# Pooled attention with a bilinear expert layer: eight blocks transposed on TensorE, half of the weight magnitudes on ScalarE

## The chip, the cores and the metric

One core of a Trainium2 chip runs the whole program. The metric is device time in microseconds, the median of the runs of one kernel.

## The reference

Attention over B, H, S, D = 4, 8, 1152, 64 with queries averaged in pairs (576 per head), then a bilinear layer on 2304 tokens of 512 features:

```python
q_pool = q.reshape(B, H, S // 2, 2, D).mean(axis=3)
scores = q_pool @ k.transpose(0, 1, 3, 2) / sqrt(D)
attn = exp(scores - max(scores)); attn = attn / (sum(attn) + 1e-09)
x = (attn @ v), heads side by side        # 2304 x 512
out = ((x @ w_a) * (x @ w_b)) @ w_out     # 512 -> 1536 -> 512
```

The layer's three weights are taken in a raw form of 64-bit words (two 32-bit words for each number), out of which the kernel makes the number itself.

## The kernel before, in words

**Attention.** Heads go in 16 pairs (two heads on the two halves of the 128 partitions), four pairs to a batch. A pass works on one pair; in batch 0 a pass takes only the even or the odd half of its queries. A pass is cut into blocks of 128 queries of one head (an even pass has 4 blocks, an odd one 5 with the rest of 64 queries). For a block: TensorE makes the scores (`qk`, L657 in f32 for the first batches, L660 from f16 halves later), VectorE scales them out of PSUM into `s` and takes the maximum (`sm_max`, L692), ScalarE takes the exponential with its sum (`sm_exp`, L699), VectorE the reciprocal of the sum (L703, L709), ScalarE divides and rounds to f16 (`sm_hi`, L712), VectorE makes the f16 remainder (`sm_lo`, L716), and SP issues a DMA transpose of both halves into `pt` (`transpose`, L722). Two blocks make a unit: TensorE multiplies `pt` by the split v (`pv`, L752), ScalarE copies the result out of PSUM (`x_copy`, L761).

**Weights.** 36 tiles (12 column groups f, each of w_a, w_b and w_out) are loaded (`w_load`, L539), their high word made a magnitude on ScalarE (`w_abs`, L545), the low word converted on ScalarE (`w_tail`, L558), the sign put in on POOL (`w_sign`, L562) and the two joined on VectorE (`w_join`, L569). For w_a and w_b a maximum over the tile gives the scale: VectorE `w_max` (L551) ahead of the join, a shift `w_mag` (L577), a sum over partitions on TensorE (`w_sum`, L583), the scale (L586) and its reciprocal (L591). Then the tile is split into two f16 parts (`w_hi`, L607, and `w_lo`, L611). All of this belongs to the first passes.

**The MoE stage.** For each of 9 token tiles and each f, TensorE multiplies x with w_b and w_a into `ab0` or `ab1` (`moe_mm`, L830; the same two PSUM tiles under the names `acc0` and `acc1` take the second product, `moe_o`, L856), ScalarE and VectorE form the product g (L837, L842), and g is split (L847, L850) for the second product. Tile 0 needs all four even passes and its weights.

**What sets the order.** Every step is added with its engine, its tiles read and written; the order of each engine's list is written out as numbers in ORDERS, one list for each of TensorE, VectorE, ScalarE, POOL and SP. Each engine goes through its list strictly in order.

Of the kernel before, what the change touches and what calls it, by code (L numbers as in the profile page):

```python
# [10 lines left out]
I32 = mybir.dt.int32  # L11
# [17 lines left out]
REMN = 64  # L29
N_WHOLE, TWO_ROUNDS = 2, (0,)  # L30
# [55 lines left out]
    ),  # L86
    (
# [215 lines left out]
def kernel(  # L303
# [46 lines left out]
    vsc = T("vsc", [128, NPAIR, 3])  # L350
    vb = T("vb", [128, B, 2])
    wmx = T("wmx", [128, NF, 2])
    wal = T("wal", [128, NF, 2])
    wsc = T("wsc", [128, 2, NF, 2])
    cc = T("cc", [128, B, NF, 2])

# [292 lines left out]
    def sbuf(i):  # L649
        return i % NS  # L650
# [429 lines left out]
```

## Time and profile before

| | us |
|---|---|
| median of 3 runs | 851.35 |
| lowest, highest run | 850.94, 855.6 |
| the profiled execution's own time | 852.03 |
| its span, first to last instruction | 849.8 |

The profile page gives busy time by engine, and forty equal slices (21.25 us each) in tenths of busy time; PEclk is TensorE's granted clock in tenths of full speed (0.5 is 1.2 GHz, full is 2.4 GHz). PE is TensorE, PEld its weight load, DVE VectorE, ACT ScalarE, POOL GpSimd, SP SyncE. L12 is line 12 of the kernel.

### The profile page before, as it was taken

The page shows a single profiled execution, that of the slowest core. Times are in us where ns is not written, and L with a number is a line of the kernel's source. Part 1 is how long each engine was busy: PE and PEld are TensorE (multiplying, and loading weights), DVE is VectorE, ACT ScalarE, POOL GpSimd, SP SyncE. Part 2 cuts the span into 40 slices and gives each one's busy share as a digit, 9 for nine tenths or more (in the row PEclk, how much of TensorE's full clock was granted, in tenths as well). Part 3 has the DMA queues.
Part 4 walks back from the last instruction along what each step waited for, and adds up shares of the span by engine and source line. Part 5 has one row for each costly group of instructions (what it writes and reads, how often), then busy time and mean ns, then how long its engine had stood idle before and what let it go on. Part 6 is the DMA issues. An engine that isn't in the chain of part 4 may idle for free.

```text
span 849.8 us, 21268 instructions
## 1 busy us (share of the span) xinstructions
PE 771.8 (91%) x8832; PEld 591.2 (70%) x8832; DVE 644.9 (76%) x1240; ACT 580.9 (68%) x929; POOL 255.1 (30%) x230
## 2 busy tenths in 40 slices
PE   4665546999999999999999999999999999999998
PEld 2343324676767777778777777787788778888886
DVE  5999999987988889899999999999866744132110
ACT  5798888877778778888888788777756644233222
POOL 3666677651240022302051113111301321201203
PEclk8755767999999999999999999999999999999999
DMA  8999899999999999999999999996965743300100
GB/s 286 233 246 263 225 222 231 270 180 228 204 208 196 192 217 188 196 191 207 161 215 195 189 193 171 168 200 142 182 159 111 116 93 57 57 27 1 25 1 25
DMA packets 353664, 141.76 MB, mean 167 GB/s; under 512 B 338208, under 2 KB 340256, under 8 KB 353568
## 3 DMA queue, kind: packets, MB, share of 16 engines
q1 hardware_dynamic: 353568, 140.40, 81.5%
q8 instruction: 69, 1.13, 0.5%
q14 instruction: 27, 0.22, 0.1%
HBM read 50.72 MB, written 4.72 MB: 65 GB/s over the span
## 4 chain that ended last, share of the span: by engine, by line
PE 53%; DVE 2%; DMA 1%; issue 1%; ACT 0%
PE ab L830 24%; PE ab L856 14%; PE sps L660 8%; PE xps L752 7%; DMA pt<-p 1%; DVE p L716 1%; DVE s L692 1%; DVE g L842 0%; ACT g L837 0%; PE xps L485 0%; DVE vs L518 0%; DVE vmx L481 0%; DVE o L862 0%; PE xps L418 0%; DVE st L709 0%
## 5 line engine op out<-in xcount | busy, mean ns | idle before, releaser
L830 PEld LDWEIGHTS <-wab 128*128 128x128 f16 x2592 | 252.4, 98 | 35.2 <-issue 2.3
L830 PE MATMUL ab<-xt,wab 128*128 128x256 f16 x2304 | 262.3, 274 | 3.2 <-DVE g L842 3.2
L716 DVE SCALAR_TENSOR_TENSOR p<-s,st,p 128x1152 f16<-128x1152 f32 x144 | 206.7, 1439 | 20.1 <-ACT p L712 19.4
L712 ACT ACTIVATE p<-s,st 128x1152 f16<-128x1152 f32 x144 | 178.4, 1248 | 44.8 <-DVE st L709 13.5
L699 ACT ACTIVATE s<-s,st 128x1152 f32<-128x1152 f32 x144 | 179.6, 1248 | 34.6 <-DVE s L692 34.4
L850 POOL TENSOR_TENSOR gl<-g,gh 128x256 fp32r<-128x256 f32 x108 | 94.0, 877 | 328.9 <-ACT gh L847 295.0
L657 PE MATMUL sps<-k,q 64*128 64x512 f32 (+3 forms) x448 | 117.5, 620 | 56.5 <-DVE s L692 36.6
L856 PE MATMUL ab<-wo,gh 128*128 128x512 f32 x432 | 140.0, 405 | 1.7 <-DVE g L842 1.7
L657 PEld LDWEIGHTS sps<-k,q 64*128 64x128 f32 (+1 forms) x448 | 54.0, 210 | 118.8 <-issue 62.9
L752 PE MATMUL xps<-pt,vs 128*64 128x128 f16 (+1 forms) x4320 | 127.4, 219 | 6.6 <-DMA pt<-p 3.8
L752 PEld LDWEIGHTS <-vs 128*64 128x64 f16 x4320 | 117.8, 113 | 19.3 <-issue 16.0
L837 ACT ACTIVATE g<-ab,cc 128x256 f32<-128x256 f32 (+1 forms) x144 | 55.6, 416 | 97.4 <-PE ab L830 97.2
L692 DVE TENSOR_SCALAR_CACHE_REDUCE s<-sps,ksc 128x1152 f32<-128x1152 f32 x72 | 101.0, 1411 | 12.0 <-PE sps L660 11.2
L842 DVE SCALAR_TENSOR_TENSOR g<-ab,cc,g 128x256 f32<-128x256 f32 (+1 forms) x144 | 56.0, 412 | 70.4 <-ACT g L837 70.3
L692 DVE TENSOR_SCALAR_CACHE_REDUCE s<-sps 128x1152 f32<-128x1152 f32 x72 | 96.8, 1349 | 7.7 <-PE sps L657 7.1
L856 PEld LDWEIGHTS ab<-wo,gh 128*128 128x128 f32 x432 | 77.8, 188 | 20.1 <-ACT g L837 1.5
L856 PE MATMUL ab<-wo,gl 128*128 128x512 f32 x216 | 85.5, 396 | 0.0
L847 ACT ACTIVATE gh<-g 128x256 fp32r<-128x256 f32 x108 | 43.4, 411 | 48.5 <-PE ab L856 47.7
L660 PE MATMUL sps<-k,q 64*128 64x512 f16 (+3 forms) x624 | 65.4, 341 | 0.0
L660 PEld LDWEIGHTS <-q 64*128 64x128 f16 (+1 forms) x720 | 36.6, 97 | 39.9 <-issue 7.4
L562 POOL TENSOR_SCALAR xt<-xt 128x512 f16<-128x512 f32 x22 | 53.9, 2449 | 22.0 <-ACT xt L558 17.0
L856 PEld LDWEIGHTS ab<-wo,gl 128*128 128x128 f32 x216 | 40.6, 188 | 10.1 <-POOL gl L850 0.4
(99 smaller groups left out, 626.2 us busy)
## 6 DMA issues: line engine op xcount, KB each, us to landing
k<-in_k_dram SPq DMA_DIRECT2D x19, 576.0 KB, 4.8
vraw<-in_v_dram SPq DMA_DIRECT2D x19, 576.0 KB, 4.7
xt<-in_w_ab_dram SPq DMA_DIRECT2D x15, 512.0 KB, 4.8
qraw<-in_q_dram SPq DMA_DIRECT2D x12, 576.0 KB, 4.7
out_dram<-o SPq DMA_DIRECT2D x16, 256.0 KB, 2.5
xt<-in_w_out_dram SPq DMA_DIRECT2D x7, 512.0 KB, 4.4
g<-in_w_ab_dram SPq DMA_DIRECT2D x5, 512.0 KB, 5.1
pt<-p SPq DMA_TRANSPOSE x144, 5.5
```

Source lines behind the costliest of these rows:

```text
L657: nc.tensor.matmul(out, q, k, start=True, stop=True)
L660: nc.tensor.matmul(out, q[:, hq], k[:, hk], start=(hq, hk) == (0, 0), stop=(hq, hk) == (1, 0))
L692: nc.vector.tensor_scalar(out=s_t[sbuf(i)], in0=sps[:, at:at + S], scalar1=-1.0 / 16.0 if u is None else ksc[:, u, 4:5], scalar2=None, op0 ...
L699: nc.scalar.activation(out=s, in_=s, func=AF.Exp, scale=-1.0, bias=t[:, 0:1], accum_out=t[:, 1:2])
L712: nc.scalar.activation(out=p_t[pbuf(i)][:, 0], in_=s_t[sbuf(i)], func=AF.Copy, scale=st_t[i % NST][:, 3:4])
L716: nc.vector.scalar_tensor_tensor(out=p[:, 1], in0=s, scalar=st_t[i % NST][:, 3:4], in1=p[:, 0], op0=ALU.mult, op1=ALU.subtract)
L752: nc.tensor.matmul(xps[half(e), at:at + w], vs[:, c, e, hv], pt[:, hp, c, c0:c0 + w], start=(c == 0 and n == 0), stop=(c == NCH - 1 and n ...
L830: nc.tensor.matmul(dst if t < 8 else dst.rearrange("p (b n) -> p b n", b=B), wab[:, f, 1 - m, a, c], moe_x(t, b, c), start=(n == 0), stop= ...
L837: nc.scalar.activation(out=g_t[:, f, c], in_=ab[j][:, 1, c], func=AF.Copy, scale=cc[:, b, f, 0:1])
L842: nc.vector.scalar_tensor_tensor(out=g, in0=ab[j][:, 0, c], scalar=cc[:, b, f, 1:2], in1=g, op0=ALU.mult, op1=ALU.mult)
L850: nc.gpsimd.tensor_tensor(out=gl_t[j], in0=g_t[:, f], in1=gh_t[j].bitcast(F32), op=ALU.subtract)
L856: nc.tensor.matmul(acc[u], g[:, us], wo[:, f, a], start=(first and n == 0), stop=(last and n == 2))
```

## The change

1. The blocks of the first two passes (two head pairs, even halves: 8 blocks) have no `sm_hi`, `sm_lo` and DMA transpose. The undivided exponentials `s` are transposed in 128 x 128 pieces on TensorE into `acc0` and `acc1` (9 pieces a block, in groups of 4, or of 2 where the last pieces of two blocks go together), and split from PSUM: ScalarE `tr_hi`, VectorE `tr_lo`. The division follows behind p times v: the reciprocals of the sums are put on the diagonal of a 128 x 128 tile (`r_diag`, ScalarE), spread over the partitions by a matmul (`r_wide`), and multiplied in (`r_mul`, VectorE). `x_copy` then takes 128 columns at a time for these passes.
2. The weight magnitude is taken behind the join. For even f a VectorE reduction (maximum of magnitudes), for odd f a ScalarE pass that sums the magnitudes. The shift of the maxima is gone.
3. An identity is made on POOL once (`unity`).
4. All five order lists are new.

```diff
+N_PE = 2
-    def w_max(f, m, n):
-        z = z_t[zi(n)]
-        nc.vector.tensor_scalar(
-            out=z, in0=z, scalar1=2.0 ** -126, scalar2=None, op0=ALU.max, op1=ALU.max, accum_out=wmx[:, f, m:m + 1]
-        )
+    def w_mag(f, m, n):
+        if on_act(f):
+            nc.scalar.activation(out=w_dst(f, m, 0), in_=w_src(m, n), func=AF.Abs, accum_out=wmx[:, f, m:m + 1])
+        else:
+            z = z_t[zi(n)]
+            nc.vector.tensor_reduce(
+                out=wmx[:, f, m:m + 1], in_=z, axis=AX.X, op=ALU.max, apply_absolute_value=True
+            )
-    def w_mag(f):
-        nc.vector.tensor_scalar(
-            out=wal[:, f].bitcast(I32), in0=wmx[:, f].bitcast(I32), scalar1=3, scalar2=None, op0=ALU.logical_shift_left
-        )
...
+    def tr_pe(chunks, j):
+        for n, (i, c) in enumerate(chunks):
+            nc.tensor.transpose(acc[j][:, 128 * n:128 * n + 128], s_t[sbuf(i)][:, 128 * c:128 * c + 128], ident)
+    def tr_hi(chunks, j):
+        nc.scalar.activation(out=tr_dst(chunks, 0), in_=tr_src(chunks, j), func=AF.Copy, scale=P_SCALE)
+    def tr_lo(chunks, j):
+        nc.vector.scalar_tensor_tensor(
+            out=tr_dst(chunks, 1), in0=tr_src(chunks, j), scalar=P_SCALE, in1=tr_dst(chunks, 0),
+            op0=ALU.mult, op1=ALU.subtract,
+        )
+    def r_diag(i, e):
+        nc.scalar.activation(out=diag[e], in_=ident, func=AF.Copy, scale=st_t[i % NST][:, 3:4])
+    def r_wide():
+        for e in range(2):
+            nc.tensor.matmul(
+                xps[half(e), 256:384], one.broadcast_to([128, 64]), diag[e], start=True, stop=True
+            )
+    def r_mul(j, x0):
+        x = x32[j][:, x0:x0 + 128]
+        nc.vector.tensor_tensor(out=x, in0=x, in1=xps[:, 256:384], op=ALU.mult)
...
+        if ps_.pe:
+            e = blocks[i].head
+            add("ACT", 0.19, i - 3, r_diag, (i, e), r=[t + "r", "g0"], w=[f"g{1 + e}"])
+            return
         add("ACT", 1.15, i - 3.5, sm_hi, (i,), r=[s, t + "r"], w=[p + "h"])
```

What stands ahead of the first MoE step in the lists, before and after. VectorE, ahead of the first `moe_g`: `sm_max` 25 and 23, `sm_lo` 23 and 13, `w_max` 22 and none, shifts 11 and none, `w_join` 31 and 30, `w_lo` 18 and 18, reductions none and 10, `tr_lo` none and 20, `r_mul` none and 4. ScalarE, ahead of the first `moe_a`: `sm_exp` 24 and 22, `sm_hi` 23 and 13, `w_abs` and `w_tail` 32 and 30 each, `w_hi` 28 and 26, `x_copy` 4 and 6, `tr_hi` none and 20, `r_diag` none and 8, magnitudes none and 8. TensorE, ahead of the first `moe_mm`: `qk` entries 25 and 23, `pv` 8 and 8, `tr_pe` groups none and 20, `r_wide` none and 4. SP issues 144 and 136 transposes in all.

## Rows read from the trace of the kernel before

**Rows 1.** The page: span, TensorE's share, then its slices, clock and DMA.

```profile
span 849.8 us, 21268 instructions
PE 771.8 (91%) x8832; PEld 591.2 (70%) x8832; DVE 644.9 (76%) x1240; ACT 580.9 (68%) x929; POOL 255.1 (30%) x230
...
PE   4665546999999999999999999999999999999998
...
PEclk8755767999999999999999999999999999999999
DMA  8999899999999999999999999996965743300100
```

**Rows 2.** Busy time by stretch: start:end us, length, then engines (instructions), clock, DMA.

```profile
0.00:150.00 150.00, 84.91 (x651) 51.89 (x652) 134.08 (x274) 118.71 (x175) 97.91 (x55) 0.69 0.98 244
150.00:210.00 60.00, 54.42 (x715) 40.50 (x714) 50.45 (x97) 46.85 (x72) 23.35 (x18) 0.97 1.07 228
210.00:780.00 570.00, 567.54 (x7047) 444.33 (x7041) 452.63 (x855) 399.49 (x647) 117.76 (x137) 1.00 0.85 159
```

**Rows 3.** TensorE's timeline where the MoE stage starts: start us, us, instruction.

```profile
143.33 3.86 PE L657 MATMUL sps<-k,q 64*128 64x512 f32 x10 [3.69 <-DVE s L692]
147.12 1.48 PE L830 MATMUL ab<-xt,wab 128*128 128x256 f16 x12
```

**Rows 4.** Waits from 0 to 160 us: total us, times, longest.

```profile
PE sps L657 <- DVE s L692: 34.6, 17, 3.7
...
ACT xt L558 <- DMA xt<-in_w_ab_dram: 4.6, 1, 4.6
...
PE xps L752 <- DMA pt<-p: 3.1, 3, 1.8
```

**Rows 5.** VectorE's groups from 0 to 150 us: busy us, mean ns, idle before.

```profile
L692 DVE TENSOR_SCALAR_CACHE_REDUCE s<-sps 128x1152 f32<-128x1152 f32 x25 | 33.7, 1348 | 2.8 <-PE sps L657 2.6
L716 DVE SCALAR_TENSOR_TENSOR p<-s,st,p 128x1152 f16<-128x1152 f32 x22 | 31.7, 1446 | 0.8 <-ACT p L712 0.7
...
L551 DVE TENSOR_SCALAR_CACHE_REDUCE o<-o 128x512 f32<-128x512 f32 x9 | 6.1, 676 | 3.9 <-ACT o L545 3.9
...
L481 DVE TENSOR_REDUCE vmx<-vraw 128x1 f32<-128x1152 f32 x4 | 5.4, 1340 | 0.0
...
L577 DVE TENSOR_SCALAR wal<-wmx 128x2 int32<-128x2 int32 x10 | 4.5, 454 | 0.0
...
L551 DVE DVE_READ_ACCUMULATOR o<-o 128x1 f32 x9 | 0.7, 82 | 0.0
```

**Rows 6.** ScalarE's groups from 0 to 150 us.

```profile
L699 ACT ACTIVATE s<-s,st 128x1152 f32<-128x1152 f32 x24 | 29.9, 1246 | 7.2 <-DVE s L692 7.2
L712 ACT ACTIVATE p<-s,st 128x1152 f16<-128x1152 f32 x23 | 28.3, 1244 | 5.8 <-DVE st L709 4.4 <-issue 1.4
...
L545 ACT ACTIVATE o<-xt 128x512 f32<-128x512 f32 x9 | 5.8, 649 | 2.1 <-DMA xt<-in_w_ab_dram 2.1
...
L699 ACT ACTIVATION_READ_ACCUMULATOR s<-s,st 128x1 f32 x24 | 4.5, 187 | 0.0
...
L761 ACT ACTIVATE x<-xps 128x256 f32<-128x256 f32 x4 | 1.4, 361 | 0.0
```

**Rows 7.** Single lines that read PSUM, whole span: ns min/median/max.

```profile
L864 ACT ACTIVATE o<-ab x9: 575/598/601, 258.8 to 845.4; 128x512 f32<-128x512 f32 x9
...
L862 DVE COPY o<-ab x9: 674/689/692, 256.8 to 846.1; 128x512 f32<-128x512 f32 x9
...
L842 DVE SCALAR_TENSOR_TENSOR g<-ab,cc,g x144: 274/475/485, 153.5 to 829.1; 128x256 f32<-128x256 f32 x96, 128x64 f32<-128x64 f32 x48
```

**Rows 8.** TensorE's timeline: one pair of scores and one rest, full clock.

```profile
99.67 2.20 PE L657 MATMUL sps<-k,q 64*128 64x512 f32 x10
...
152.61 0.48 PE L657 MATMUL sps<-k,q 64*128 64x128 f32 x2
```

**Rows 9.** POOL's timeline at the start.

```profile
5.62 0.72 POOL L408 TENSOR_TENSOR q<-qraw 128x256 f32<-128x256 f32 x1 [5.18 <-DMA qraw<-in_q_dram]
```

More of the change, by code (lines that the diff above doesn't have):

```diff
@@ L352 @@
     wmx = T("wmx", [128, NF, 2])
-    wal = T("wal", [128, NF, 2])
     wsc = T("wsc", [128, 2, NF, 2])
@@ L387 @@
     kzf = [x.bitcast(F16).rearrange("p (a n) -> p a n", a=2) for x in kz]
+    ident, diag = g_t[:, 0, 0:128], [g_t[:, 1 + e, 0:128] for e in range(2)]
     pl = Plan()
@@ L547, in w_abs, with on_act @@
         )
-    def w_max(f, m, n):
-        z = z_t[zi(n)]
-        nc.vector.tensor_scalar(
-            out=z, in0=z, scalar1=2.0 ** -126, scalar2=None, op0=ALU.max, op1=ALU.max, accum_out=wmx[:, f, m:m + 1]
-        )
+    def on_act(f):
+        return f % 2 == 1
+    def w_mag(f, m, n):
[6 more added lines that the diff above has]
+            )
     def w_tail(n):
@@ L574, in w_ones @@
         nc.vector.memset(one, 1.0)
-    def w_mag(f):
-        nc.vector.tensor_scalar(
-            out=wal[:, f].bitcast(I32), in0=wmx[:, f].bitcast(I32), scalar1=3, scalar2=None, op0=ALU.logical_shift_left
-        )
     def w_sum(f):
-        nc.tensor.matmul(sums, one.broadcast_to([128, 128]), wal[:, f], start=True, stop=True)
+        nc.tensor.matmul(sums, one.broadcast_to([128, 128]), wmx[:, f], start=True, stop=True)
     def w_scale(f):
         nc.vector.tensor_scalar(
-            out=wsc[:, 1, f], in0=sums, scalar1=2.0 ** -100, scalar2=2.0 ** -14, op0=ALU.max, op1=ALU.mult
+            out=wsc[:, 1, f], in0=sums, scalar1=2.0 ** -100, scalar2=2.0 ** -15, op0=ALU.max, op1=ALU.mult
         )
@@ L625, in prep_w @@
             add("ACT", 0.55, key, w_abs, (n,), r=[rw], w=[z])
-            if m < 2:
-                add("DVE", 0.6, key, w_max, (f, m, n), w=[z, f"wmx{f}{m}"])
             add("ACT", 0.555, key, w_tail, (n,), w=[rw + "l"], r=[rw])
@@ L630, in prep_w @@
             add("DVE", 0.68, key, w_join, (n,), r=[rw, rw + "l"], w=[z], port=True)
+            if m < 2:
+                last = [f"z{NZ + m}"] if f == NF - 1 else []
+                last += ["raw2"] if f == NF - 2 else []
+                if on_act(f):
+                    add("ACT", 0.66, key, w_mag, (f, m, n), r=[z], w=[f"wmx{f}{m}", f"w{f}{m}h"] + last)
+                else:
+                    add("DVE", 0.6, key, w_mag, (f, m, n), r=[z], w=[f"wmx{f}{m}"])
             if m == 1:
-                add("DVE", 0.07, key, w_mag, (f,), r=[f"wmx{f}0", f"wmx{f}1"], w=[f"wal{f}"])
-                add("PE", 0.2, key - 5, w_sum, (f,), r=[f"wal{f}", "ones"], w=["xps"])
+                add("PE", 0.2, key - 5, w_sum, (f,), r=[f"wmx{f}0", f"wmx{f}1", "ones"], w=["xps"])
                 add("DVE", 0.07, key - 5, w_scale, (f,), r=["xps"], w=[f"wsd{f}"])
@@ L725, in transpose, with unity, tr_dst @@
         )
+    def unity():
+        nc.gpsimd.memset(ident, 0.0)
+        nc.gpsimd.affine_select(
+            out=ident, in_=ident, compare_op=ALU.not_equal, fill=1.0, base=0, pattern=[[-1, 128]], channel_multiplier=1
+        )
+    def tr_pe(chunks, j):
+        for n, (i, c) in enumerate(chunks):
+            nc.tensor.transpose(acc[j][:, 128 * n:128 * n + 128], s_t[sbuf(i)][:, 128 * c:128 * c + 128], ident)
+    def tr_dst(chunks, hl):
+        i, c = chunks[0]
+        c0 = 128 * blocks[i].slot
+        if chunks[1][0] == i:
+            return pt[:, hl, c:c + len(chunks), c0:c0 + 128]
+        return pt[:, hl, c, c0:c0 + 256]
@@ new lines, in tr_src @@
+    def tr_src(chunks, j):
+        x = acc[j][:, 0:128 * len(chunks)]
+        return x.rearrange("p (c n) -> p c n", n=128) if chunks[1][0] == chunks[0][0] else x
+    def tr_hi(chunks, j):
[5 more added lines that the diff above has]
+        )
@@ new lines, in r_diag, with moved @@
+    def r_diag(i, e):
[4 more added lines that the diff above has]
+                xps[half(e), 256:384], one.broadcast_to([128, 64]), diag[e], start=True, stop=True
+            )
+    def r_mul(j, x0):
+        x = x32[j][:, x0:x0 + 128]
+        nc.vector.tensor_tensor(out=x, in0=x, in1=xps[:, 256:384], op=ALU.mult)
+    def moved(ps_, i0, u):
+        slots = [blocks[i].slot for i in (i0, i0 + 1)]
+        parts = [[(i, c + d) for d in range(4)] for i in (i0, i0 + 1) for c in (0, 4)] + [[(i0, 8), (i0 + 1, 8)]]
+        for n, chunks in enumerate(parts):
+            j = n % 2 if u % 2 == 0 else (n + 1) % 2
+            of = sorted(set(i for i, _ in chunks))
+            names = [f"pt{blocks[i].slot}x{chunks[0][1]}" for i in of]
+            add("PE", 0.05 + 0.17 * len(chunks), i0 - 6, tr_pe, (chunks, j), r=[f"s{sbuf(i)}" for i in of] + ["g0"], w=[f"acc{j}"])
+            add("ACT", 0.08 + 0.107 * len(chunks), i0 - 3.5, tr_hi, (chunks, j), r=[f"acc{j}"], w=[x + "h" for x in names])
+            add("DVE", 0.1 + 0.14 * len(chunks), i0 - 3.5, tr_lo, (chunks, j), r=[f"acc{j}"] + [x + "h" for x in names], w=[x + "l" for x in names])
+        return [f"pt{t}x{c}{hl}" for t in slots for c in (0, 4, 8) for hl in "hl"]
@@ L758, in pv, with x_copy, unit @@
                     )
-    def x_copy(j, at, x0, w):
-        nc.scalar.activation(out=x32[j][:, x0:x0 + w], in_=xps[:, at:at + w], func=AF.Copy, scale=1.0 / P_SCALE)
-    def unit(slots, at, w, key):
+    def x_copy(j, at, x0, w, scale):
+        nc.scalar.activation(out=x32[j][:, x0:x0 + w], in_=xps[:, at:at + w], func=AF.Copy, scale=scale)
+    def unit(slots, at, w, key, parts):
         runs = [128 * t for t in slots] if len(slots) > 1 else [128 * slots[0], 128 * slots[0] + w]
-        add("PE", 0.04 + 1.49 * w / 128, key - 9, pv, (runs, at, w), r=[f"pt{t}" for t in slots] + ["vsh", "vsl"],
+        add("PE", 0.04 + 1.49 * w / 128, key - 9, pv, (runs, at, w), r=[f"pt{t}" for t in slots] + ["vsh", "vsl"] + parts,
             w=["xps"], mode=2)
@@ L769, in leave @@
         j = ps_.jx
-        add("ACT", 0.072 + 0.192 * w / 256, key - 4, x_copy, (j, at, x0, w), r=["xps"],
-            w=[f"x32{j}{c}" for c in range(x0 // 64, (x0 + w) // 64)])
+        add("ACT", 0.072 + 0.192 * w / 256, key - 4, x_copy, (j, at, x0, w, P_SCALE ** -2 if ps_.pe else 1.0 / P_SCALE),
+            r=["xps"], w=[f"x32{j}{c}" for c in range(x0 // 64, (x0 + w) // 64)])
+        if ps_.pe:
+            add("DVE", 0.22, key - 4, r_mul, (j, x0), r=["xps"], w=[f"x32{j}{c}" for c in range(x0 // 64, (x0 + w) // 64)])
     def x_parts(p, j, which, hl):
@@ L926, in __init__ @@
             self.whole = b > 0
+            self.pe = n < N_PE
             self.split = b >= N_WHOLE
@@ L978 @@
     add("DVE", 0.2, -30, w_ones, (), w=["ones"])
+    add("POOL", 0.8, -30, unity, (), w=["g0"], port=False)
     prep_qk(passes[0], -20)
@@ L1002, in attend @@
                 prep_vmax(nxt.p, nxt.parts[0] == "even", ps_.end - 4)
-            unit(slots, at, w, i - 1)
+            parts = moved(ps_, i - 2, r) if ps_.pe else []
+            unit(slots, at, w, i - 1, parts)
+            if ps_.pe:
+                add("PE", 0.3, i - 9, r_wide, (), r=["g1", "g2", "ones"], w=["xps"], mode=2)
+                leaving = [(at, XE + at, 128)]
             for span in leaving:
```

285 rows, old and new, of the table ORDERS are left out of this document.

## The prediction

> **What bounds the kernel now.** I read the page first. TensorE is busy for 771.8 of 849.8 us, and its granted clock is below full only in the first seven of the forty slices [rows 1]. So the next view is busy time by stretch [rows 2]. From 210 to 780 us TensorE works 567.5 of 570 us at full clock: whatever it has to do there is paid in full, and nothing else in that stretch can shorten the run. The first 150 us are different: TensorE is busy 84.9 us at a mean clock of 0.69, VectorE 134.1 us and ScalarE 118.7 us. This is the start-up, in which 36 weight tiles are joined and split while the first head pairs are attended. It ends when the first matmuls of the MoE stage enter, at 147.1 us, behind a scores product that was itself waiting for VectorE [rows 3]. From there TensorE is full (54.4 of 60 us in the stretch that follows).
>
> Who holds the start-up is in the waits: TensorE waits 34.6 us for VectorE's scaled copy with maximum, in 17 waits, but only 3.1 us for transposed probabilities, and ScalarE 4.6 us for weight loads [rows 4]. The DMA engines are nearly full there too (0.98), but hardly anybody waits for them: the bound is VectorE, 89% busy, with ScalarE at 79% behind it.
>
> So the time is (when the MoE stage starts) + (work that TensorE still has to do). The profiled execution took 852.03 us for its span of 849.8, and the median of the runs is 851.35; I take differences from that execution and apply them to the median.
>
> **The change, part by part.**
>
> *Eight blocks without DMA transpose.* For each, VectorE loses a sm_lo of 1.446 us [rows 5] and ScalarE a sm_hi of 1.244 us [rows 6]. In their place come 20 groups (16 of 512 columns, 4 of 256) that are read from PSUM: tr_lo on VectorE, tr_hi on ScalarE. Nearest rows, also PSUM to SBUF: VectorE 0.689 us for 512 columns and 0.475 for 256 (the median, which is the 256-column form), ScalarE 0.598 for 512 [rows 7] and 0.361 for 256 [rows 6]. So tr_lo costs 16 x 0.689 + 4 x 0.475 = 12.9 us against 8 x 1.446 = 11.6, and tr_hi 16 x 0.598 + 4 x 0.361 = 11.0 us against 10.0: neither engine gains by this part alone. The division that moves behind p times v adds 4 r_mul of 128 columns to VectorE, between 0.08 (a one-column reading) and 0.475 us: I take 0.31, 1.2 us. On ScalarE 8 r_diag of 128 columns lie between 0.187 and 0.361: I take 0.28, 2.2 us. The copies out of PSUM are now 8 of 128 columns instead of 4 of 256: about 8 x 0.28 - 4 x 0.361 = 0.8 us.
>
> *TensorE.* 72 transposes of 128 x 128 and four r_wide. No row shows a transpose. The nearest is the f32 product on 128 columns, two instructions in 0.48 us [rows 8]. A transpose costs between 0.1 us (if loads and streams overlap) and 0.48; I take one instruction of the pair, 0.24 us, together 17 us, and 7 to 35 for the range. All of it is ahead of the first MoE step in TensorE's list, so it falls into the 65 us in which TensorE idles by 150 us and is costed at nothing. If that cover were gone (half clock, see the rivals), it would be paid in full.
>
> *DMA.* Eight transposes leave SP's queue. Its engines move less, but since the waits for them are a few us, I count nothing for it; weight loads may land earlier, which is a reason for a gain beyond my value, none for a loss.
>
> *Weight magnitude.* VectorE loses 24 w_max of 0.676 + 0.082 us and 12 shifts of 0.454 us: 18.2 + 5.4. It gains 12 reductions of 512 columns. The reduction over 1152 columns took 1.340, as long per column as the instruction it replaces, so I take 0.676 (0.60 by simple proportion): 8.1 us. ScalarE gains 12 magnitudes, each a 512-column pass of 0.649 and an accumulator read of 0.187: 10.0 us. The magnitude is now behind the join in its chain (sign on POOL, join, magnitude), so scales come later for a tile; what hides this is that tiles are joined long before the MoE stage needs them.
>
> *unity on POOL* stands first in its list, where POOL waits 5.18 us for the first queries [rows 9]: nothing.
>
> *Sum over all parts.* VectorE: -11.6 - 18.2 - 5.4 + 12.9 + 8.1 + 1.2 = -13.0 us. ScalarE: -10.0 + 11.0 + 2.2 + 10.0 + 0.8 = +14.0 us. Work moves from the engine that bounds the start-up to the one behind it.
>
> *Order.* The lists are written anew, so what counts is the work that stands ahead of the first MoE step, by the counts that the text gives with the diff. VectorE: 2 sm_max of 1.43 fewer (-2.9), 10 sm_lo fewer (-14.5), 22 w_max (-16.7) and 11 shifts (-5.0) gone; 20 tr_lo (+12.9), 10 reductions (+6.8), 4 r_mul (+1.2) added: -18.2 us, 134.1 becomes 115.9. ScalarE: 2 sm_exp with readings fewer (-2.9), 10 sm_hi fewer (-12.4), 2 each of w_abs, w_tail and w_hi fewer (-3.9 at 0.649); 20 tr_hi (+11.0), 8 r_diag (+2.2), 8 magnitudes (+6.7), 6 small copies for 4 (+0.2): +0.9 us, 118.7 becomes 119.6. The two are now level.
>
> When does the MoE stage start? If one engine alone sets it, at VectorE's 89%, ScalarE's 119.6 us give 134 us, 16 earlier. If the two keep the joint rate that they have now (252.8 us of work in 150), 235.5 us take 139.7: 10.3 earlier. I take the second, since a block passes from one to the other several times and two level engines wait on each other more than one full and one slack engine. Against this, two entries of scores (one pair of 2.20 and one rest of 0.48 at full clock [rows 8]) are no longer done in the start-up but in the full stretch: +2.7. **Net -7.6 us: 851.35 - 7.6 = 843.7 us.** By the profiled execution itself it would be 844.4.
>
> **The rivals.**
>
> *A, a larger gain.* One engine sets the pace, or the lighter DMA lets weights land early: start at 134 us, -16 + 2.7 = -13, 838 us or somewhat less. For it: the DMA share of 0.98. Against: those small waits.
>
> *B, no change.* ScalarE's idle 31 us of 150 are not VectorE's fault, and with no less work on it the stage starts where it did. Then the two moved scores cost 2.7 and what VectorE saves becomes idle: 851 to 854. For it: ScalarE's work ahead of the MoE stage does not fall. Against: the waits that rank first are for VectorE.
>
> *C, slower: two PSUM buffers.* All 20 groups pass through the same two tiles, acc0 and acc1. A group's buffer is free again only after four transposes, the tr_hi and the tr_lo, and each engine keeps its order: a tr_lo that waits holds back the sm_max behind it, and so TensorE's next scores. If each group leaves VectorE idle for 1 us, the start comes 20 us later than forecast: 851.35 - 7.6 + 20 = 863.8. It decides from 7.6 / 20 = 0.38 us per group on. Against: VectorE's list puts a sm_max, a join or a magnitude between most groups.
>
> *D, slower: TensorE at half clock becomes the bound.* In the start-up TensorE already runs for long stretches at 1.2 GHz (a tenth between 5 and 10 is a mixture of the two levels, 1.2 and 2.4 GHz) [rows 1]. Its 84.9 us at 0.69 are 58.6 us at full clock, 117 at half; less the moved scores (5.4 at half), with transposes of 17 us, that is 129 us, and if the 34.6 us of waits for VectorE stay, the stage starts at 164: +14 + 2.7, 868 us. For it: the clock's digit is 5 in slices three and four already. Against: TensorE will idle less, not more. The Trainium skill, TensorE: Matmul & The Clock Gate, section on the PE-mode transpose, speaks for D: it says that the full clock does not engage for matmuls in transpose mode, and gives about 275 ns for one of bf16 in a kernel, by which 72 would take 20 us (an estimate from that page). No run here shows either so far.
>
> **How the numbers follow.** The forecast of -7.6 gets 0.48, A 0.16, B 0.19, C 0.12, D 0.05. A change of under 0.5% (4.3 us, 847.1 to 855.6) is about what a measurement of this kernel cannot tell from none. All of A and the forecast lie below it: 0.64 faster; B is within it: 0.19; C and D are above: 0.17. The likeliest case's own range is 838 to 847, by the two ways to reckon the start and by TensorE's bounds. To hold the time 8 times in 10 the range takes A's value and B: 836 to 854; out remain C, D and the far end of A.
>
> **What would show it.** Right: the first MoE matmuls at about 140 us instead of 147 (137 to 143); VectorE near 116 us busy by then and ScalarE near 120; TensorE's waits for sm_max well below 34.6 us; the stretch behind as full as before. The new rows should read: tr_lo 0.69, tr_hi 0.60, a transpose near 0.24 us. Wrong: if the stage starts at 147 or later with VectorE idle in front of tr_lo, it is C; with ScalarE at 85% and more and VectorE waiting for it, B; with a clock near 0.5 and TensorE busy throughout, D. If the start is earlier but the time is not, then TensorE must idle later, in the 60 us after the start, where more weight tiles than before are still to be split.

## The result, and the profile after

The changed kernel takes 841.03 us (median of 4 runs, 836.85 to 841.74) against 853.48 for the kernel before on the same chips; ratio 0.9848, 95% interval 0.9806 to 0.989. The forecast was faster, 843.7 us, 0.9% below the median; it came out 1.5% below. Measured again beside the experiments, the kernel before took 851.69, 851.87 and 850.98 us (medians of 25, 31 and 9 runs), so against those the gain is 10 to 11 us and not 12.4. The profiled execution is the fastest of the runs, 836.85 us for a span of 835.1, so of the 14.7 us between the spans of the two traces a few are not the change's; the medians decide.

The page of the changed kernel: span, busy share, TensorE's slices (20.9 us each), clock and DMA, against [rows 1].

```profile
span 835.1 us, 21457 instructions
...
PE 773.5 (93%) x8920; PEld 595.4 (71%) x8920; DVE 637.0 (76%) x1208; ACT 588.4 (70%) x975; POOL 261.0 (31%) x232
...
PE   6765659999999999999999999999999999999998
...
PEclk9986669999999999999999999999999999999999
DMA  7569999999999999999999999798679735000100
```

TensorE is full from the seventh slice on, one slice earlier, and its clock is 9, 9 and 8 in the first three slices, where it was 8, 7 and 5. Its timeline where the MoE stage starts, against [rows 3]:

```profile
128.29 2.20 PE L667 MATMUL sps<-k,q 64*128 64x512 f32 x10 [1.47 <-DVE s L702]
130.43 5.42 PE L901 MATMUL ab<-xt,wab 128*128 128x256 f16 x48
```

The stage starts at 130.4 us, 16.7 earlier, again behind scores that waited for VectorE. Busy time in three stretches, cut at that start, 63 us behind it, and at the end (columns as in [rows 2]): first the changed kernel, then the kernel before cut in the same way.

```profile
0.00:130.43 130.43, 81.30 (x701) 51.97 (x701) 117.41 (x232) 114.34 (x200) 92.63 (x55) 0.82 0.81 225
130.43:193.43 63.00, 61.97 (x814) 47.23 (x814) 55.67 (x104) 55.99 (x91) 31.20 (x21) 1.00 1.09 228
193.43:835.10 641.67, 630.22 (x7409) 496.24 (x7407) 463.87 (x874) 418.06 (x686) 137.19 (x157) 1.00 0.77 146
```

```profile
0.00:147.12 147.12, 82.03 (x624) 49.28 (x624) 131.24 (x268) 115.83 (x171) 95.11 (x54) 0.69 0.97 245
147.12:210.12 63.00, 57.42 (x745) 43.23 (x746) 53.42 (x103) 49.73 (x76) 26.27 (x19) 0.97 1.08 226
210.12:849.80 639.68, 632.40 (x7472) 498.64 (x7466) 460.24 (x871) 415.36 (x683) 133.76 (x159) 1.00 0.76 143
```

These six lines hold the account. A span is the start, plus TensorE's busy time behind it, plus its idle time behind it. Before: 147.1 + 689.8 + 12.9. After: 130.4 + 692.2 + 12.5. So -16.7 at the start, +2.4 for work behind it, -0.4 of idle time, -14.7 in all. Note VectorE and ScalarE ahead of the start: 0.89 and 0.79 busy before, 0.90 and 0.88 after.

The new groups up to 130.4 us: on VectorE tr_lo (two forms), one of the magnitudes, r_mul; on ScalarE tr_hi (two forms), r_diag, one of the magnitudes and its reading. Columns as in [rows 5].

```profile
L762 DVE SCALAR_TENSOR_TENSOR pt<-ab,pt 128x512 f16<-128x512 f32 x16 | 10.7, 681 | 0.1
...
L562 DVE TENSOR_REDUCE wmx<-o 128x1 f32<-128x512 f32 x4 | 2.7, 676 | 0.0
...
L762 DVE SCALAR_TENSOR_TENSOR pt<-ab,pt 128x256 f16<-128x256 f32 x4 | 1.6, 412 | 0.0
...
L778 DVE TENSOR_TENSOR x<-x,xps 128x128 f32<-128x128 f32 x4 | 1.1, 283 | 0.5 <-ACT x L830 0.5
```

```profile
L759 ACT ACTIVATE pt<-ab 128x512 f16<-128x512 f32 x16 | 9.0, 589 | 0.3 <-PE ab L745 0.3
...
L768 ACT ACTIVATE g<-g,st 128x128 f32<-128x128 f32 x8 | 3.2, 394 | 0.0
L559 ACT ACTIVATE wab<-o 128x512 f16<-128x512 f32 x4 | 2.5, 620 | 0.1
...
L759 ACT ACTIVATE pt<-ab 128x256 f16<-128x256 f32 x4 | 1.5, 372 | 0.0
...
L559 ACT ACTIVATION_READ_ACCUMULATOR wab<-o 128x1 f32 x4 | 0.8, 190 | 0.0
```

VectorE sat idle 0.1 us ahead of tr_lo and ScalarE 0.3 ahead of tr_hi: neither waits for the two PSUM buffers. TensorE does, a little; two of its waits from 0 to 160 us, against [rows 4]:

```profile
PE sps L667 <- DVE s L702: 24.6, 12, 5.2
...
PE ab L745 <- DVE pt L762: 5.3, 4, 2.1
```

The transposes, by their line (duration ns min/median/max), and two of the pieces in which they run on TensorE's timeline:

```profile
L745 PE MATMUL ab<-g,s x72: 272/273/476, 13.0 to 53.9; 128*128 128x128 f32 x72
```

```profile
18.03 1.10 PE L745 MATMUL ab<-g,s 128*128 128x128 f32 x8
...
24.18 1.09 PE L745 MATMUL ab<-g,s 128*128 128x128 f32 x8
```

A record is 273 ns long, but eight of them take 1.10 us: by that one starts every (1.10 - 0.27) / 7 = 0.12 us.

### The profile page after: what moved, and what is told of

It reads as the page before. It is cut to its first block, busy times and chain, and to the rows that moved or that the text cites. A ratio compares the mean times of both kernels' runs of the same rounds, so it can differ in the third digit from the quotient of the medians.

```text
span 835.1 us, 21457 instructions
## 1 busy us (share of the span) xinstructions
PE 773.5 (93%) x8920; PEld 595.4 (71%) x8920; DVE 637.0 (76%) x1208; ACT 588.4 (70%) x975; POOL 261.0 (31%) x232
## 4 chain that ended last, share of the span: by engine, by line
PE 52%; DVE 9%; DMA 2%; issue 2%; ACT 1%; DVEq 0%; ACTq 0%
PE ab L901 25%; PE ab L927 12%; PE sps L670 7%; PE xps L821 6%; DVE p L726 3%; DVE s L702 2%; DMA pt<-p 2%; PE sps L667 1%; ACT p L722 0%; DVE vmx L486 0%; ACT g L908 0%; DVE g L913 0%; DVE k L442 0%; DVE xt L863 0%; DVE q L450 0%
## 5 line engine op out<-in xcount | busy, mean ns | idle before, releaser
L921 POOL TENSOR_TENSOR gl<-g,gh 128x256 fp32r<-128x256 f32 x108 | 96.7, 900 | 371.9 <-ACT gh L918 317.2
L726 DVE SCALAR_TENSOR_TENSOR p<-s,st,p 128x1152 f16<-128x1152 f32 x136 | 195.0, 1438 | 14.8 <-ACT p L722 14.1
L722 ACT ACTIVATE p<-s,st 128x1152 f16<-128x1152 f32 x136 | 169.6, 1250 | 46.3 <-DVE st L719 15.6
L667 PE MATMUL sps<-k,q 64*128 64x512 f32 (+3 forms) x448 | 110.7, 587 | 36.0 <-DVE s L702 25.1
L821 PEld LDWEIGHTS <-vs 128*64 128x64 f16 x4320 | 116.3, 112 | 18.2 <-issue 15.9
L667 PEld LDWEIGHTS sps<-k,q 64*128 64x128 f32 (+1 forms) x448 | 51.7, 198 | 94.1 <-issue 56.6
L573 POOL TENSOR_SCALAR xt<-xt 128x512 f16<-128x512 f32 x22 | 53.9, 2449 | 20.9 <-ACT xt L569 19.9
L927 PEld LDWEIGHTS ab<-wo,gl 128*128 128x128 f32 x216 | 40.6, 188 | 10.1 <-POOL gl L921 0.3
```

Of the source, the lines that this page charges most:

```text
L667: nc.tensor.matmul(out, q, k, start=True, stop=True)
L722: nc.scalar.activation(out=p_t[pbuf(i)][:, 0], in_=s_t[sbuf(i)], func=AF.Copy, scale=st_t[i % NST][:, 3:4])
L726: nc.vector.scalar_tensor_tensor(out=p[:, 1], in0=s, scalar=st_t[i % NST][:, 3:4], in1=p[:, 0], op0=ALU.mult, op1=ALU.subtract)
L821: nc.tensor.matmul(xps[half(e), at:at + w], vs[:, c, e, hv], pt[:, hp, c, c0:c0 + w], start=(c == 0 and n == 0), stop=(c == NCH - 1 and n ...
L921: nc.gpsimd.tensor_tensor(out=gl_t[j], in0=g_t[:, f], in1=gh_t[j].bitcast(F32), op=ALU.subtract)
L927: nc.tensor.matmul(acc[u], g[:, us], wo[:, f, a], start=(first and n == 0), stop=(last and n == 2))
```

## The experiments

The theory after the result: VectorE, and close behind it ScalarE, set when the MoE stage starts; TensorE and DMA have room. Rivals: TensorE's full clock in the first 42 us moved the start; TensorE's added work costs; the rewritten order, not the moved steps, is what gained.

### More work on one engine

E1, the VectorE magnitudes of the weights and the first four maxima of v twice (a `tensor_reduce` done again writes the same result):

```diff
-            nc.vector.tensor_reduce(
-                out=wmx[:, f, m:m + 1], in_=z, axis=AX.X, op=ALU.max, apply_absolute_value=True
-            )
+            for _ in range(2):
+                nc.vector.tensor_reduce(
+                    out=wmx[:, f, m:m + 1], in_=z, axis=AX.X, op=ALU.max, apply_absolute_value=True
+                )
...
+        for _ in range(2 if p < NP else 1):
             nc.vector.tensor_reduce(out=vmx[:, p:p + 1], in_=vraw, ...)
```

> The changed kernel with every VectorE magnitude of the weights and the first four maxima of v done twice: 12 x 0.67 + 4 x 1.34 = 13.4 us more work on VectorE in the start-up, results unchanged. If VectorE sets the pace of the start-up, the first MoE matmuls move from 130 us to 141 to 145, and the time by about the same 11 to 15 us, to 852 to 856. If the two engines share the pace, by half of it, 847 to 849. If the start came earlier because of TensorE's full clock, little: 841 to 844.

E2, the same for the ScalarE pass of `w_mag` and for `r_diag` (`for _ in range(2):` ahead of each).

> The changed kernel with every ScalarE magnitude and every r_diag done twice: 12 x 0.82 + 8 x 0.39 = 13 us more work on ScalarE in the start-up, results unchanged. If VectorE alone sets the pace, ScalarE (114 of 130 us busy) has room for most of it: 841 to 845. If the two engines share the pace: half of it, 847 to 849. If ScalarE has become the bound: 852 to 856.

E3, `for _ in range(2):` ahead of `nc.tensor.transpose` in `tr_pe`.

> The changed kernel with each of the 72 transposes on TensorE done twice: 72 x 0.27 = 20 us more TensorE work in the first 55 us, results unchanged. If TensorE has room there, as the prediction costed it, 840 to 844. If TensorE's time in the start-up is on the path, each group of four comes 1.1 us later and 20 groups give up to 20 us: 850 to 861.

Measured: E1 850.44, E2 852.11, E3 845.14 us, against the changed kernel's 841.03, which was taken at another time: the kernel before took 851.69 us beside these three and 853.48 beside the changed kernel, so by the ratios to it each of the three differences is 2 to 3 us larger than the ones below. Up to the start of the MoE stage, E1, E2 and E3 in turn:

```profile
0.00:140.48 140.48, 88.24 (x700) 56.94 (x701) 126.69 (x245) 115.16 (x199) 90.81 (x55) 0.72 0.77 215
```

```profile
0.00:138.39 138.39, 84.87 (x700) 53.69 (x701) 118.22 (x232) 122.87 (x224) 92.07 (x55) 0.78 0.76 215
```

```profile
0.00:134.43 134.43, 89.90 (x772) 60.72 (x772) 118.28 (x232) 115.25 (x200) 93.81 (x55) 0.80 0.80 223
```

In E1 VectorE is busy 9.3 us longer ahead of the start (126.7 against 117.4); that moves the start by 10.1 us, and the time by 9.4. In E2 ScalarE is busy 8.5 us longer (122.9 against 114.3); that moves the start by 8.0 us, and the time by 11.1. So each of the two engines is now a bound by itself; the 12% that ScalarE was idle was no room. In E1 VectorE is 126.7 / 140.5 = 0.90 busy at the start, in E2 ScalarE 122.9 / 138.4 = 0.89. Of the three expectations VectorE's held nearly, and ScalarE's came out at the one for a bound. E3 was expected to add 20 us to TensorE and added 9.3 (TensorE's busy time in all, 782.8 against 773.5), as a spacing of 0.13 us has it. It does not look free: start and time are 4 us later, for 9.3 us on TensorE less than half. Behind the start E3's trace idles 17 us instead of 12.5, but the two spans differ by 9.4 us and the medians by 4.1, so this part is not shown.

### TensorE's clock by itself

E4, the kernel before with transposes that nobody reads, ahead of the scores:

```diff
+        if len(warm) < 18:
+            warm.append(0)
+            for n in range(4):
+                nc.tensor.transpose(acc[0][:, 128 * n:128 * n + 128], ident, ident)
```

> The kernel before with 72 transposes of a constant tile that nobody reads, four ahead of each of the first 18 score entries; an identity is made at the start on POOL. It gives the kernel before the changed kernel's TensorE activity without its relief of VectorE. If VectorE sets the pace: the granted clock of the first 42 us rises from 0.78 towards 1.0, the MoE stage still starts at 145 to 148 us, 850 to 854. If the full clock is what moved the start, it starts at 135 to 140 and the time is 842 to 846. If transposes leave the clock at half, the clock does not rise and the start comes later: 855 and more.

Measured: 852.09 us (ratio to the kernel before 1.0012, 0.999 to 1.0035). The first 42.5 us of the kernel before, of E4 and of the changed kernel in turn, then E4 up to its MoE start:

```profile
0.00:42.50 42.50, 21.95 (x160) 13.05 (x160) 31.68 (x62) 27.77 (x37) 21.64 (x16) 0.78 0.97 259
0.00:42.50 42.50, 25.18 (x176) 16.38 (x178) 29.55 (x59) 25.52 (x34) 18.43 (x17) 0.89 0.95 260
0.00:42.50 42.50, 27.57 (x226) 17.95 (x226) 32.31 (x69) 33.59 (x64) 26.42 (x20) 0.99 0.65 231
```

```profile
0.00:147.38 147.38, 88.62 (x696) 56.61 (x696) 130.46 (x269) 116.22 (x171) 98.21 (x56) 0.79 1.00 245
```

The granted clock rose from 0.69 to 0.79 over the start-up, nearly the changed kernel's 0.82, and the MoE stage started at 147.4 instead of 147.1. In this trace a TensorE at a higher clock gives no earlier start: VectorE is about as busy as before, 130.5 us, 0.89. The theory that the clock moved the start falls as far as the clock rose: 0.89 and not 0.99 in the first 42.5 us. How much of the rise is the transposes' is less sure, since the granted clock differs between executions: over the whole span it is 0.944 in the trace of the kernel before, 0.961 in E4's, and 0.952 and 0.957 in the medians of their timed runs.

### The parts, and the order

A part that is undone changes the list of steps, so the order has to be made again. The next four have all five lists made by the same local search.

> The steps of the kernel before, with its five order lists made anew by a local search over moves within a list (10 million trials, the same for this kernel and the next three). If the rewritten order is what gains, 838 to 845. If the moved work gains, as the prediction has it, this one has only what a longer search still finds: 846 to 852, MoE start at 142 to 147 us.

> The changed kernel without its transposes (the eight blocks go by sm_hi, sm_lo and DMA as before): only the magnitudes are moved; order lists by the same search. By the two doubling runs (0.70 us of time for a us on VectorE, 0.85 for one on ScalarE) moving 15.5 us off VectorE and 10 onto ScalarE is worth -10.9 + 8.5 = -2.4 us against the searched order of before. If the magnitudes carry the gain of the change, 8 us and more below it, and the transposes alone little.

> The changed kernel with the magnitudes as before (maximum ahead of the join and shifts, all on VectorE): only the eight blocks are transposed on TensorE; order lists by the same search. By the prediction's terms VectorE gains 2 us of work and ScalarE 4, so with nothing else it is 2 to 5 us above the searched order of before. If taking eight DMA transposes and their latency out of the start-up is what gains, it is 5 us and more below it, and engine work is not the whole account.

> Both parts, the steps of the changed kernel, order lists by the same search. If the parts add up, its distance from the searched order of before is the sum of the two single parts' distances; if one relieves what the other loads (VectorE and ScalarE level out), it is more than the sum. At or below the changed kernel's 841: 836 to 842.

The edit of E6 is `N_PE = 0` (and no `unity`); that of E7 puts back `w_max` and the shift ahead of the join; E5 is the kernel before and E8 the changed kernel, with other numbers in ORDERS. E5, E6 and E8 came out above what was expected of them; E7 came out 6.0 us below E5, its second case, in which engine work is not the whole account. E8 has the changed kernel's steps and takes 6 us more. So a second set keeps the last 59 to 75% of each of the changed kernel's lists word for word, and searches the start-up alone.

> The steps of the kernel before on the changed kernel's order: the last 59 to 75% of each list is the changed kernel's word for word, and only the start-up, where its steps differ, was ordered anew by local search. It asks whether the changed kernel's late order carries part of the gain. If it does: TensorE idles 11 us behind the start-up as in the changed kernel, and the time is 843 to 848. If the gain is in the start-up's steps: 849 to 853.

> Magnitudes moved, no transposes on TensorE; late part of the lists that of the changed kernel, start-up ordered anew by the same search. By the fully searched pair (854.9 against 852.9) the magnitudes alone give nothing: within 3 us of the run with the order alone. If they are half of the gain, 5 to 7 us below it.

> Eight blocks transposed on TensorE, magnitudes as before; late part of the lists that of the changed kernel, start-up ordered anew by the same search. By the fully searched pair (846.9 against 852.9) 5 to 8 us below the run with the order alone, with TensorE's idle time in the start-up some 12 us smaller and a DMA share near 0.8 there. If it was the luck of that pair's orders, within 3 us of it.

> All steps of the changed kernel; late part of the lists its own, start-up ordered anew by the same search. If the changed kernel's 841 rests on its steps, 838 to 843. If its start-up order is one that suits the chip by chance, 844 to 848, as the fully searched one was.

| steps | searched throughout: us, ratio to before | changed kernel's late order: us, ratio to before |
|---|---|---|
| as before | E5: 852.89, 1.002 (1.0 to 1.0041) | E9: 847.59, 0.996 (0.9945 to 0.9974) |
| magnitudes | E6: 854.92, 1.0044 (1.002 to 1.0067) | E10: 847.8, 0.9959 (0.9945 to 0.9973) |
| transposes | E7: 846.94, 0.995 (0.993 to 0.997) | E11: 848.63, 0.9965 (0.9951 to 0.9979) |
| both | E8: 847.48, 0.9952 (0.9932 to 0.9972) | E12: 840.42, 0.9867 (0.9835 to 0.9899) |

Two things hold in both columns. Both parts together are worth 0.7 to 0.9% by the ratios to the kernel before, against the same kind of order without them (852.89 - 847.48 = 5.4 us; 847.59 - 840.42 = 7.2). And the magnitudes alone gain nothing (+2.0 and +0.2 us), not even the 2.4 us worked out from the two doubling runs; that ScalarE has to take what VectorE gives up would account for it. The transposes alone are not settled: -6.0 us in one column, +1.0 in the other. Nor is what the magnitudes add to the transposes: +0.5 (E7 to E8) and -8.2 (E11 to E12). So which part earns the gain stays open, and with it whether the eight DMA transposes that fall away matter by themselves. E10's and E12's expectations held; of E11's the second case came, the luck of the other pair's orders. What E9 has with no step changed, 0.4%, is order alone. Its time is within what was expected if the late order carries part of the gain, but TensorE idles 17.5 us behind its start, not as little as in the changed kernel (12.5). E5, with another order of the same steps, is no faster than the kernel before.

How can an order cost so much? E5 and E12, in three stretches cut as above:

```profile
0.00:134.69 134.69, 71.94 (x612) 44.61 (x613) 120.01 (x245) 105.46 (x156) 91.38 (x51) 0.73 0.99 248
134.69:197.69 63.00, 55.61 (x667) 41.62 (x667) 58.37 (x112) 53.22 (x81) 33.67 (x19) 0.99 1.06 222
197.69:852.90 655.21, 638.86 (x7556) 503.90 (x7553) 470.27 (x885) 420.77 (x693) 133.20 (x162) 1.00 0.75 144
```

```profile
0.00:124.38 124.38, 80.81 (x691) 52.29 (x691) 110.08 (x219) 109.15 (x192) 83.38 (x52) 0.78 0.81 225
124.38:187.38 63.00, 60.63 (x712) 45.39 (x711) 58.93 (x111) 58.22 (x96) 33.23 (x19) 1.00 1.09 227
187.38:834.00 646.62, 633.05 (x7522) 499.14 (x7519) 469.27 (x881) 421.66 (x689) 140.95 (x162) 1.00 0.77 146
```

E5 starts the MoE stage at 134.7 us, 12.4 earlier than the kernel before, by putting attention work behind the start, and is no faster: TensorE's busy time behind the start is 694.5 us instead of 689.8, and its idle time there 23.7 instead of 12.9. Of these 10.9 us more, 1.8 lie in the 63 us that follow the start, in which VectorE is 0.93 busy with the work left over (0.85 before), and 9.1 later; what causes those was not tried. An early start is worth only what is not paid back so. E12 starts earliest of all, at 124.4 us, idles 16 behind it, and ends level with the changed kernel: its time does not hang on one order of the start-up, and how much a better one could still give is not shown.

So the start alone does not order these runs. E6 starts at 129.7 us, E9 at 137.5 and E8 at 136.2; in turn:

```profile
0.00:129.65 129.65, 73.19 (x603) 45.02 (x603) 111.96 (x201) 106.13 (x166) 83.24 (x48) 0.71 0.99 254
129.65:192.65 63.00, 56.98 (x688) 42.85 (x687) 58.18 (x105) 55.27 (x92) 35.98 (x19) 1.00 1.01 211
192.65:851.10 658.45, 638.17 (x7546) 501.85 (x7543) 471.76 (x889) 424.12 (x698) 141.90 (x163) 1.00 0.76 145
```

```profile
0.00:137.48 137.48, 70.77 (x613) 44.05 (x613) 122.39 (x244) 108.65 (x160) 89.34 (x50) 0.78 0.97 244
137.48:200.48 63.00, 60.27 (x805) 46.21 (x806) 59.59 (x121) 53.97 (x84) 34.71 (x22) 1.00 1.12 232
200.48:847.00 646.52, 631.75 (x7418) 496.89 (x7414) 464.72 (x878) 418.91 (x686) 136.73 (x159) 1.00 0.76 145
```

```profile
0.00:136.19 136.19, 85.73 (x700) 55.53 (x700) 121.57 (x230) 119.91 (x208) 94.33 (x56) 0.78 0.81 226
136.19:199.19 63.00, 57.97 (x733) 43.34 (x732) 55.34 (x100) 49.61 (x80) 25.89 (x17) 0.99 0.97 207
199.19:847.00 647.81, 632.75 (x7490) 500.19 (x7488) 465.53 (x878) 418.23 (x688) 136.32 (x161) 1.00 0.76 144
```

E6 starts as early as the changed kernel and spans 16 us more, because TensorE has 695.2 us of work and 26.3 of idle time behind the start. E9, with no step changed, starts 9.6 us earlier than the kernel before. And the two columns gain in two ways: E12 starts 13.1 us earlier than E9, but E8 starts 1.5 later than E5 and gains by 3.8 us less work and 3.6 less idle time behind the start.

## Why the prediction was right, and where it was off

**What bounds the kernel** was right in the main: TensorE full at full clock behind the start, the start-up bound by VectorE with ScalarE behind it. E1 and E2 show that each of the two engines moves the start. E4 shows no gain from a higher clock of TensorE, and E3 that more TensorE work costs less than half of itself. Whether the lighter DMA gave anything was not tried by itself.

**Prices** held. tr_lo cost 16 x 0.681 + 4 x 0.412 = 12.5 us (12.9 forecast), tr_hi 16 x 0.589 + 4 x 0.372 = 10.9 (11.0), r_mul 1.1 (1.2). r_diag was mis-sized: 0.394 us, above the upper end of 0.361 that was taken from a copy out of PSUM without a scale per partition. The magnitudes came as priced, 0.676 and 0.62 + 0.19.

**The sums of engine work** held less well than 115.9 forecast and 117.4 measured on VectorE look. The forecast starts from work up to 150 us, 2.9 us behind the start. Cut at the start in both traces, VectorE fell from 131.2 to 117.4 us, by 13.8 and not 18.2, and ScalarE from 115.8 to 114.3, where +0.9 was forecast. Over the whole span, by [rows 1] and the page above, VectorE lost 7.9 us of busy time and not 13.0, and ScalarE gained 7.5 and not 14.0. One reason can be seen in VectorE's timeline in the trace of the kernel before: records overlap, so a record's length is more than what it adds to busy time. Behind each of these two joins of 0.68 us the next instruction starts 0.60 us after it:

```profile
143.20 0.68 DVE L569 SCALAR_TENSOR_TENSOR wab<-wab,xt 128x512 int32<-128x512 int32 x1
143.80 0.68 DVE L569 SCALAR_TENSOR_TENSOR o<-o,wab 128x512 int32<-128x512 int32 x1
144.41 0.39 DVE L792 TENSOR_SCALAR xt<-xt,vsc 128x512 f16<-128x512 f16 x1
```

**Work moved behind the start** was forecast at 2.7 us; TensorE's busy time there grew by 2.4.

**The step that failed** is the one that turns work into a start: "if the two keep the joint rate that they have now ... 139.7: 10.3 earlier". The sign that was given with it, first MoE matmuls at 137 to 143 us, failed: they came at 130.4, 16.7 earlier. Part of this is a slip: 139.7 is reckoned from 150 us and not from the start at 147.1, so the start that goes with 10.3 earlier is 136.8. The larger part is the joint rate, which makes the start 10.3 us earlier and not 16.7. The other reckoning, by the busier engine at VectorE's 89%, has 16 us earlier, and with it -13 us, rival A's value; the spans of the two traces differ by 14.7, the medians by 12.4, or by 10 to 11 with the later runs of the kernel before, which is between the forecast and A. The runs show why the joint rate was wrong: in all the kernels here the busier of the two engines is 0.86 to 0.90 busy when the MoE stage starts, whether the other is at 0.79 (before, E4, E7, E9) or also at 0.88 (after, E8, E12). Level engines did not wait on each other more.

Luck had a part too: the sum has no term for the order as such, and an order made anew for the same steps moved the time by +1.0 us in E5 and by -3.4 in E9.

**Transposes** were taken at 0.24 us, 17 us together, with 0.1 us, which no row showed, as the lower end; they cost 0.12 to 0.13 us each, about 9 us, so the lower end was the better guess. "Costed at nothing" was not quite right: as much again cost 4 us in E3. Whether the first 72 cost as much was not tried.

**The rivals.** Of A, the first leg, one engine that sets the pace, is what the shares of busy time bear out; the second, that the lighter DMA lets weights land early, is not shown: its share ahead of the start fell from 0.97 to 0.81, and the transposes alone gained 6.0 us once and lost 1.0 once. B (ScalarE holds the start) is wrong as put, since the start moved, but E2 shows that ScalarE is now a bound of its own. C (two buffers) is wrong: TensorE waits 5.3 us for tr_lo, VectorE hardly at all. D (half clock) is wrong: the clock is 0.99 in the first 42.5 us instead of falling, with 54 of the 72 transposes in them, and in E4, whose only addition on TensorE is transposes among the same scores, it is 0.89 there and not below the 0.78 of the kernel before. The Trainium skill, TensorE: Matmul & The Clock Gate, section on the PE-mode transpose, has it that the full clock does not engage for transposes; these two traces disagree. The 275 ns that this section of the Trainium skill gives for one of bf16 in a kernel is near the record of 273 ns for one of f32 here, and not the spacing.

**What was not foreseen** is how much the order itself is worth. The prediction counted what stands ahead of the MoE stage in the new lists, and took all of that as the change's gain. Of the 10.6 us that E12 gains on the kernel before as measured beside it (850.98), 3.4 are from order with no step changed (E9) and 7.2 from both parts on a like order; in the fully searched pair the order costs 1.0 and both parts give 5.4. How much of the gain belongs to each part is not settled.

## What to carry to other kernels

Where two engines feed a third, reckon the start of the third's stage by the busier one at the share at which it is busy now, not by their sum; once the two are level, a microsecond more on either costs most of itself, as E1 and E2 show. Before crediting an edit with a gain, give the unedited steps an order made in the same way: here that alone moved the time by +1 and by -3 us. Count what an earlier start leaves to be done behind it, in busy and in idle time of the engine that is full there; E6 gave back all of its early start so. And before subtracting two amounts of work, cut both traces at the same event.

## What the runs showed of the hardware that was not expected

A transpose of a 128 x 128 f32 tile on TensorE has a record of 273 ns, but eight in a row take 1.10 us, and 72 more of them add 9.3 us. The first 42.5 us of the changed kernel, with 54 such transposes between f32 scores, ran at a granted clock of 0.99, against 0.78 for the same stretch of the kernel before (TensorE was busy 27.6 of the 42.5 us there, 21.9 before). With the same transposes E11 had 0.84 there, and E9 without any 0.88, so the transposes do not keep the clock at half, and that they raise it is not shown. A ScalarE copy of 128 columns from SBUF with a scale per partition took 394 ns, more than one of 256 columns from PSUM with a constant scale, 361 [rows 6]. Records of VectorE overlap: in the kernel before they add up to 724.7 us over the whole span, and the engine is busy 644.9.
